# w2 laid out as eight rows on 128 partitions, five on 64 and one on 32, in a gated attention and FFN decode kernel

## The chip, the cores and the metric

The kernel runs on one core of one Trainium2 chip. The metric is the device time of one execution in microseconds; the median of three runs is 344.23 us (344.19 to 344.23). The profile is of one execution, taken by the hardware profiler.

## What is computed

One decode step for two sequences (B = 2, one new token each). An attention block with 32 heads of 128 over a cache of 4,096 keys and values, and a ReLU feed-forward block, are mixed by a gate:

```python
g = sigmoid((x * gate_w).sum(-1, keepdims=True))          # x: [2, 1, 512]
q = x @ wq                                                # wq: [512, 4096]
p = softmax(q k^T / sqrt(128))                            # k_cache, v_cache: [2, 32, 4096, 128]
a = (p v) @ wo                                            # wo: [4096, 512]
b = relu(x @ w1) @ w2                                     # w1: [512, 1376], w2: [1376, 512]
out = g * a + (1 - g) * b
```

All arrays are bf16. The inputs are 145 MB, nearly all of it the two caches, and each byte is used once.

## The kernel before

The program is written out by hand, one list of operations per engine. A helper (`P.add`) records each operation with the markers it waits for, and `emit` (line 61) turns markers into waits on one semaphore per engine; every DMA transfer has a semaphore of its own or one shared with transfers that never overlap with it. Nothing is scheduled by a compiler: an engine does its list in order.

**The transfers.** All large loads are issued by SyncE (SP) and go through one queue (q1) in this order: w1 (line 267), wq (268), ten pieces of the key cache (272), nine of the value cache (282), wo in two parts (283, 284), then w2 (285, 290). A key or value transfer waits only until its place in SBUF has been read, and several are always under way. A transfer to 128 partitions is handled by all 16 DMA engines, eight partitions each, and adds one to its semaphore for each engine that has finished, so the waiter sees 16 when all have. x and the gate's vector (lines 265, 266) go through ScalarE's own queue.

**The attention.** For each of 64 pieces of K, VectorE transposes 32x32 blocks (`k_turn`, line 386; the first one waits for pe_h, the end of the matmuls of line 371) and TensorE adds scores into four PSUM banks (lines 407 and 197). The softmax follows over all units at once (413 to 432), then nine V jobs: GpSimd, VectorE and ScalarE spread the probabilities (`spread`, 444 to 448), TensorE does 64 or 32 matmuls (461), VectorE extracts the diagonal blocks (467, 471) into X2. `o_gather` (486 to 499) normalises, `project` (508) multiplies with wo, and DVE copies the result (511).

**The feed-forward block.** Right after the query projection `ffn_h` (line 371) computes h transposed: 11 column blocks of w1, each of 128 columns, four matmuls per block, into 22 PSUM columns. VectorE (line 375, once per sequence) applies the ReLU and the gate's (1 - g) and writes hT, 128 partitions x 11 x 2. The second product needs the same split of the 1,376 hidden units: w2's first 1,280 rows are laid as ten consecutive rows on each of 128 partitions, and the eleventh block is rows 1,248 to 1,375, one row per partition. 32 of its rows (1,248 to 1,279) are in the ten already, so GpSimd zeroes their part of hT (line 379).

w2 is loaded last, into the space of the K tiles, once the last probabilities have been spread (marker pt_8). It comes as six transfers: w2a (line 285, the eleventh block, 128 x 512 elements), then (line 290) w2b with rows 0 to 5 of each partition's ten, w2c with rows 6, 7 and half of 8, w2d with half of row 9, w2e with the other half of row 8, w2f with the rest of row 9.

The end of the program, in TensorE's order: `project` (32 matmuls, line 508), four matmuls on the eleventh block (516), `wo_sum` (540, four matmuls that add the projected attention, waiting for DVE's copy of line 511), rows 0 to 7 (516, 32 matmuls; the first waits for w2b, row 6 for w2c), two matmuls for half of row 8, and `ffn_last` (520), whose six loads of weights (202) and six matmuls (208) wait for w2d, w2e and w2f. Two copies by DVE and two by ACT (579, 581) go to out_sb, and SP and ACT send one output row each (293).

Of the kernel before, what the change touches and what calls it, by code (L numbers as in the profile page):

```python
# [3 lines left out]
dt = mybir.dt  # L4
ALU = mybir.AluOpType
ACT = mybir.ActivationFunctionType
AX = mybir.AxisListType
# [78 lines left out]
def bass_gated_mix__gqa_block_cached__dense_activation_relu__decode_kernel(  # L86
# [14 lines left out]
    sb = nc.alloc_sbuf_tensor  # L101
# [3 lines left out]
    x_sb = sb("x_sb", [3, 512], dt.bfloat16)  # L105
    xT3 = sb("xT3", [128, 4, 4], dt.bfloat16)
# [7 lines left out]
    gm = sb("gm", [128, 2], dt.float32)  # L114
# [14 lines left out]
    selx = sb("selx", [128, 56], dt.float32)  # L129
# [2 lines left out]
    s4 = sb("s4", [32, 4, 128], dt.bfloat16)  # L132
    O_sb = sb("O_sb", [32, 2, 128], dt.bfloat16)
    oW = sb("oW", [128, 32, 2], dt.bfloat16)
    hT = sb("hT", [128, 11, 2], dt.bfloat16)
    out_sb = sb("out_sb", [2, 512], dt.bfloat16)


    flat = kt[:, :, :].rearrange("p k n -> p (k n)")
    kt16 = flat.bitcast(dt.bfloat16).rearrange("p (k r n two) -> p k r n two", k=NKT, r=64, two=2)  # L140
    w1 = flat[:, 0:2752].bitcast(dt.bfloat16)
    E = flat[:, 0:2048].bitcast(dt.bfloat16)
    ET = flat[:, 4096:6144].bitcast(dt.bfloat16)
    w2f = flat[:, 0:2816].bitcast(dt.bfloat16)
    w2 = w2f.rearrange("p (r n) -> p r n", n=512)
    X2 = flat[:, 2944:4096].rearrange("p (u d) -> p u d", d=128)
# [17 lines left out]
    MISC = 7 * BANK  # L164
    G_C0 = MISC + 64
    XT_B0 = 2 * (MISC + 400)
    H_C0 = MISC + 72
    L_C0 = MISC + 96
    O_C0 = MISC + 128
    R_C0 = MISC + 256  # L170
# [4 lines left out]
    sem = {n: nc.alloc_semaphore("sem_" + n) for n in names}  # L175
# [17 lines left out]
    pool, dve, act, pe, sp = (adder(e) for e in ("pool", "dve", "act", "pe", "sp"))  # L193
# [12 lines left out]
    def held_at(e, out, lhsT, rhs, g, last):  # L206
        low = e.lower_ap
        return e.add_instruction(mybir.InstMatmult(
            start_tensor_calc=False, stop_tensor_calc=last, tile_size=(128, 32), tile_position=(0, 32 * g), ldweights=False,
            name=nc.get_next_instruction_name(), engine=mybir.EngineType.PE, ins=[low(rhs), low(lhsT)], outs=[low(out)]))  # L210
# [5 lines left out]
         waits=["c_i16z"], signal="c_i16")  # L216
# [5 lines left out]
         waits=["c_i32z"], signal="c_i32")  # L222
# [6 lines left out]
         waits=["c_s4z"], signal="c_s4")  # L229
# [2 lines left out]
    wq_in = A_wq.rearrange("(p t) n -> p (t n)", t=4)  # L232
    w1_in = B_w1.rearrange("(p t) f -> p (t f)", t=4)
    wo_in = A_wo.rearrange("(p r) n -> p (r n)", r=32)
    w2_in = B_w2[0:1280, :].rearrange("(p r) n -> p (r n)", r=10)
    k_rows = A_k_cache.rearrange("b h s d -> (b h s) d")
    v_rows = A_v_cache.rearrange("b h s d -> (b h s) d")

# [30 lines left out]
    for g, (u, halves) in enumerate(segments):  # L269
        dst = kv[:, 4, :] if len(halves) == 1 else region[:, place(g) // 2, :]  # L270
        src = unit_in(k_rows, u)[:, 16384 * halves[0]:16384 * (halves[-1] + 1)]
        sp(lambda e, g=g, dst=dst, src=src: e.dma_start(dst, src).then_inc(sem_k[g % 3], 16),
           waits=([f"kt_{last_of[g - 3]}"] if g >= 3 else ["pe_qr1"] if g == 2 else []))
    for j, (u, hf) in enumerate(jobs):
        src = unit_in(v_rows, u)
# [9 lines left out]
    sp(lambda e: e.dma_start(w2[:, 10, :], B_w2[1248:1376, :]).then_inc(sem["w2a"], 16),  # L285
       waits=[f"pt_8_{hq}" for hq in range(4)])


    for name, c0, c1 in (("w2b", 0, 3072), ("w2c", 3072, 4352), ("w2d", 4608, 4864), ("w2e", 4352, 4608), ("w2f", 4864, 5120)):
        sp(lambda e, name=name, c0=c0, c1=c1: e.dma_start(w2f[:, c0:c1], w2_in[:, c0:c1]).then_inc(sem[name], 16))  # L290

    def send(b):
# [63 lines left out]
    def q_put(g):  # L356
        b, u4 = divmod(segments[g][0], 4)
        cols = qT_ps.rearrange("p (f j s m) -> p f s j m", f=2, j=4, s=4)
        for hq in range(4):
# [2 lines left out]
                in_=cols[32 * hq:32 * hq + 32, u4 // 2, 2 * (u4 % 2):2 * (u4 % 2) + 2, :, b], func=ACT.Copy),  # L362
                waits=(["pe_q", "c_qbuf"] if g < 2 else [f"pe_sc_{last_of[g - 2]}"]), signal=f"q_{g}_{hq}")

    def ffn_h():
        for ft in range(11):
            for t in range(4):
                def fn(e, ft=ft, t=t):
                    o = t * DFF
                    cols = w1[:, o + ft:o + 1280:10] if ft < 10 else w1[:, o + 1248:o + 1376]  # L370
                    return e.matmul(psf(0, 128, H_C0 + 2 * ft, 2), lhsT=cols, rhs=xT3[:, t, 0:2], start=(t == 0), stop=(t == 3))
                pe(fn, dwaits=([(sem["w1"], 16)] if ft == 0 and t == 0 else []),
                   signal=("pe_h" if ft == 10 and t == 3 else None))
        for b in range(2):
            dve(lambda v, b=b: v.tensor_scalar(out=hT[:, :, b], in0=PSF[:, H_C0 + b:H_C0 + 22:2], scalar1=0.0,
                                               scalar2=gm[:, b:b + 1], op0=ALU.max, op1=ALU.mult),
                waits=["pe_h", "dve_gm"], signal=f"dve_h{b}")
# [72 lines left out]
    def v_unit(j):  # L450
# [4 lines left out]
        for m in range(n):  # L455
            t = m % 4
            waits, dwaits = [], []
            if m == 0:
# [4 lines left out]
                rhs=rows[:, m], start=(m < 4), stop=(m >= n - 4), tile_position=(0, 32 * t)),  # L463
               waits=waits, dwaits=dwaits, signal=(f"pe_v_{j}" if m == n - 1 else None))

    def v_extract(u):
# [4 lines left out]
        dve(lambda e: e.tensor_reduce(out=X2[:, u, :], in_=Y.rearrange("p (c d) -> p d c", c=4), axis=AX.X, op=ALU.add),  # L471
            waits=[f"dve_y{u}"], signal=f"dve_x{u}")

    def denominators():
# [8 lines left out]
    def o_gather(b, js, start, stop):  # L483
        for j in js:
            u, first, last = jobs[j][0] % 4, start and j == js[0], stop and j == js[-1]
            pe(lambda e, u=u, j=j, first=first, last=last: e.matmul(  # L486
                psf(0, 32, O_C0, 128), lhsT=selx[:, 24 - 8 * u:56 - 8 * u], rhs=X2[:, j, :], start=first, stop=last),
               waits=[f"dve_x{j}"] + (["dve_rinv", "dve_selx"] if first else []) + (["dve_O0"] if b else []),
               signal=(f"pe_O{b}" if last else None))
        if not stop:  # L490
            return
        dve(lambda v, b=b: v.tensor_scalar(out=O_sb[:, b, :], in0=psf(0, 32, O_C0, 128), scalar1=rinv[:, b:b + 1],
                                           scalar2=gb[0:32, b:b + 1], op0=ALU.mult, op1=ALU.mult),
            waits=[f"pe_O{b}", "dve_rinv", "dve_g"], signal=f"dve_O{b}")
        for dq in range(4):
            pe(lambda e, dq=dq, b=b: e.matmul(psf(0, 128, R_C0 + 32 * b, 32), lhsT=s4[:, dq, :], rhs=O_sb[:, b, 32 * dq:32 * dq + 32],
                                              start=(dq == 0), stop=(dq == 3), tile_position=(0, 0)),
               waits=([f"dve_O{b}", "c_s4"] if dq == 0 else []), signal=(f"pe_R{b}" if dq == 3 else None))
        dve(lambda v, b=b: v.tensor_copy(out=oW[:, :, b], in_=psf(0, 128, R_C0 + 32 * b, 32)), waits=[f"pe_R{b}"], signal=f"dve_oW{b}")

    def fin(g):
        return psf(32 * g, 32 * g + 2, FIN_B * BANK, 128)
# [8 lines left out]
        dve(lambda v: v.tensor_copy(out=YW, in_=psf(0, 128, WO_B * BANK, 512)), waits=["pe_wo"], signal="dve_yw")  # L511

    def ffn_f(r, first=False, groups=4):
        dw = {10: [(sem["w2a"], 16)], 0: [(sem["w2b"], 16)], 6: [(sem["w2c"], 16)]}.get(r, [])
        for g in range(groups):
            pe(lambda e, g=g: e.matmul(fin(g), lhsT=hT[:, r, :], rhs=w2[:, r, 128 * g:128 * g + 128],
                                       start=first, stop=False, tile_position=(0, 32 * g)),
               dwaits=(dw if g == 0 else []), waits=(["dve_h0", "dve_h1", "c_h10", "dve_z"] if first and g == 0 else []))

    def ffn_last():  # L520
        def load(r, g):
            pe(lambda e: load_at(e, hT[:, r, :], g))

        def mult(r, g, dw=(), signal=None):
            pe(lambda e: held_at(e, fin(g), hT[:, r, :], w2[:, r, 128 * g:128 * g + 128], g, r == 9), dwaits=dw, signal=signal)

        for r, g in ((9, 0), (9, 1), (8, 2), (8, 3)):
            load(r, g)
        mult(9, 0, dw=[(sem["w2d"], 16)])
        mult(9, 1, signal="pe_fin0")  # L530
        for g in (2, 3):
            mult(8, g, dw=([(sem["w2e"], 16)] if g == 2 else []))
        for g in (2, 3):
            load(9, g)
        mult(9, 2, dw=[(sem["w2f"], 16)])
        mult(9, 3, signal="pe_fin1")

    def wo_sum():
        for g in range(4):
# [75 lines left out]
```

## Time and profile before

| | |
|---|---|
| median of three runs | 344.23 us (344.19 to 344.23) |
| profiled execution, span | 342.9 us (342.95 from the first to the end of the last instruction) |
| around the span | the profile lists no other time for that execution; the median is 1.28 us above the span |
| bytes moved, mean rate | 145.61 MB, 425 GB/s |
| TensorE, VectorE, ScalarE, GpSimd busy | 58%, 52%, 7%, 6% |
| chain of work that ended last | DMA 68%, DVE 15%, PE 13% |

The page gives the busy share of each engine in 40 slices; the row "DMA" is the mean over the 16 DMA engines, a 9 being 90% or more. Its queue lines give packets, megabytes and the packets' time as a share of 16 engines' span: q1 is SyncE's queue, q10 ScalarE's, q8 and q14 bring instructions. The trace behind the page also has each packet (start, length, bytes, queue, but not which of the 16 engines) and, for each transfer, the 16 times at which its semaphore rose; these are called landings here. All times are from the span's start.

### The profile page before, as it was taken

To read this page: it belongs to the slowest core of one execution; us is meant where nothing else is said; L and a number is where in the kernel's file an instruction comes from. 1 tells how busy PE (TensorE), PEld (TensorE's weight loads), DVE (VectorE), ACT (ScalarE), POOL (GpSimd) and SP (SyncE) were. 2 spreads that over 40 slices of the span, in tenths; PEclk is the share of its full clock that TensorE was granted. 3 is DMA by queue.
4 is the path that set the end of the run, shared out by engine and by line. 5 is a ranking of instruction groups with operands and counts; after the bars stand their busy time and mean duration, and the time that the engine had idled before them with its cause. 6 is when DMAs were issued, how large, how long until landed. Compare 5 with 4: busy or idle time off the path is not lost.

```text
span 342.9 us, 2540 instructions
## 1 busy us (share of the span) xinstructions
PE 197.8 (58%) x1228; PEld 54.3 (16%) x972; DVE 178.5 (52%) x127; ACT 23.1 (7%) x71; POOL 19.9 (6%) x36
## 2 busy tenths in 40 slices
PE   0177329799969799699799337220706043150656
PEld 0141001111111111111111013100303011020231
DVE  2239059899789899698999562220100103020121
ACT  1040000000000000000000240000000000000000
POOL 8000000000000000000000040110100101000000
PEclk9999959989999999989999858755656756565787
DMA  8998989899998999999999999999999999998996
GB/s 348 428 489 369 482 375 482 382 474 413 438 489 367 429 443 466 392 459 390 475 420 436 461 390 420 445 466 413 443 413 445 428 428 443 413 468 382 440 401 239
DMA packets 4196, 145.61 MB, mean 425 GB/s; under 512 B 469, under 2 KB 986, under 8 KB 1242
## 3 DMA queue, kind: packets, MB, share of 16 engines
q1 hardware_dynamic: 4178, 145.46, 98.5%
q8 instruction: 8, 0.13, 0.2%
q14 instruction: 2, 0.02, 0.0%
q10 hardware_dynamic: 8, 0.00, 0.0%
HBM read 145.46 MB, written 0.00 MB: 424 GB/s over the span
## 4 chain that ended last, share of the span: by engine, by line
DMA 68%; DVE 15%; PE 13%; ACT 1%; issue 1%; POOL 0%; SPq 0%; DVEq 0%
DMA kv<-in_A_k_cache_dram 31%; DMA kv<-in_A_v_cache_dram 23%; DVE kt L386 13%; DMA kt<-in_B_w_dram 9%; PE PS L461 6%; DMA kv<-in_A_wq_dram 4%; PE PS L407 3%; PE PS L197 3%; ACT kt L428 1%; PE PS L333 1%; DVE mpad L413 1%; DVE kt L471 1%; POOL ptm L444 0%; DVE qbuf L467 0%; DVE kt L432 0%
## 5 line engine op out<-in xcount | busy, mean ns | idle before, releaser
L386 DVE STREAM_TRANSPOSE kt<-kv 128x2048 f32<-128x2048 f32 x64 | 141.2, 2274 | 22.4 <-DMA kv<-in_A_k_cache_dram 22.3
L407 PE MATMUL PS<-kt,qbuf 128*128 128x512 bf16 x256 | 105.7, 413 | 31.8 <-DVE kt L386 26.3
L197 PE MATMUL PS<-kt,qbuf 128*128 128x512 bf16 x256 | 105.1, 411 | 0.0
L461 PE MATMUL PS<-kv,ptm 128*32 128x512 bf16 x512 | 46.5, 541 | 79.0 <-DMA kv<-in_A_v_cache_dram 76.0
L467 DVE TENSOR_TENSOR qbuf<-PS,maskc 128x512 f32<-128x512 f32 x9 | 6.2, 692 | 109.0 <-PE PS L461 109.0
L407 PEld LDWEIGHTS PS<-kt,qbuf 128*128 128x128 bf16 x256 | 25.5, 100 | 139.9 <-DVE kt L386 72.7
L461 PEld LDWEIGHTS PS<-kv,ptm 128*32 128x32 bf16 x512 | 19.0, 129 | 105.1 <-issue 98.6
L444 POOL COPY ptm<-kt 32x512 bf16<-32x512 bf16 (+1 forms) x18 | 11.5, 638 | 268.7 <-DVE rsum L475 175.6
L360 ACT ACTIVATE qbuf<-PS 32x8 bf16<-32x8 bf16 x40 | 7.9, 196 | 134.2 <-PE PS L197 132.7
L448 ACT ACTIVATE ptm<-kt 32x512 bf16<-32x512 bf16 (+1 forms) x9 | 5.3, 603 | 100.1 <-PE PS L461 98.7
L471 DVE TENSOR_REDUCE kt<-qbuf 128x128 f32<-128x512 f32 x9 | 9.3, 1028 | 0.3
L428 ACT ACTIVATE kt<-PS,negm 128x512 bf16<-128x512 f32 x8 | 5.4, 696 | 30.4 <-DVE negm L424 30.4
L333 PE MATMUL PS<-kv,xTw 128*32 128x512 bf16 x32 | 3.6, 629 | 5.9 <-DMA kv<-in_A_wq_dram 5.9
L478 PE MATMUL PS<-rsum,sell 128*32 128x1 f32 x4 | 0.4, 196 | 10.1 <-DVE rsum L475 10.1
L432 DVE STREAM_TRANSPOSE kt<-kt 128x1024 bf16<-128x1024 bf16 x4 | 5.0, 1245 | 1.7 <-ACT kt L428 1.4
L348 DVE CAST qrow<-PS 128x256 bf16<-128x256 f32 x2 | 2.4, 1396 | 6.4 <-PE PS L333 6.4
L508 PE MATMUL PS<-kv,oW 128*2 128x512 bf16 x32 | 3.4, 590 | 1.4 <-DMA kv<-in_A_wo_dram 1.4
L300 PE MATMUL PS<-ident,x_sb 3*128 3x3 bf16 x4 | 0.3, 166 | 6.2 <-DMA x_sb<-in_gate_w_dram 6.2
L486 PE MATMUL PS<-kt,selx 128*32 128x128 f32 x18 | 3.4, 328 | 0.3 <-DVE kt L471 0.3
L303 DVE COPY xT<-PS 128x12 bf16<-128x12 bf16 x1 | 0.2, 169 | 6.5 <-PE PS L300 6.5
L230 POOL MEMSET ptm<- 128x4096 bf16 x1 | 3.5, 3501 | 0.0
L413 DVE TENSOR_REDUCE mpad<-PS 128x1 f32<-128x2048 f32 x1 | 2.3, 2290 | 2.1 <-PE PS L197 2.1
(64 smaller groups left out, 44.2 us busy)
## 6 DMA issues: line engine op xcount, KB each, us to landing
kv<-in_A_k_cache_dram SPq DMA_DIRECT2D x4, 4096.0 KB, 31.6
kv<-in_A_v_cache_dram SPq DMA_DIRECT2D x2, 4096.0 KB, 27.0
kv<-in_A_wq_dram SPq DMA_DIRECT2D x1, 4096.0 KB, 15.0
kv<-in_A_wo_dram SPq DMA_DIRECT2D x1, 3072.0 KB, 29.3
kt<-in_B_w_dram SPq DMA_DIRECT2D x1, 1376.0 KB, 5.8
kv<-in_A_wo_dram SPq DMA_DIRECT2D x1, 1024.0 KB, 31.3
kt<-in_B_w_dram SPq DMA_DIRECT2D x1, 768.0 KB, 31.9
kt<-in_B_w_dram SPq DMA_DIRECT2D x1, 320.0 KB, 32.3
```

The source lines that it names most:

```text
L197: return e.add_instruction(mybir.InstMatmult(start_tensor_calc=start, stop_tensor_calc=stop, tile_size=(128, 128), tile_position=(0, 0), l ...
L333: pe(lambda e, n=n, t=t: e.matmul(psf(32 * (n % 4), 32 * (n % 4) + 32, (QR_B + n // 4) * BANK, 512), lhsT=xTw[:, t, :], rhs=wq_sb[:, t, n ...
L360: act(lambda a, hq=hq: a.activation(out=qbuf[32 * hq:32 * hq + 32, g % 2, :, :, 32 + 32 * hq], in_=cols[32 * hq:32 * hq + 32, u4 // 2, 2 * ...
L386: dve(lambda v: v.transpose(out=dst, in_=pairs[:, h, 64 * rr:64 * rr + 64]), waits=([f"pe_sc_{i - NKT}"] if i >= NKT else ["pe_h"] if i == ...
L407: return e.matmul(args[0], lhsT=args[1], rhs=args[2], start=first, stop=last)
L413: dve(lambda v: v.tensor_reduce(out=mpad[:, 0:1], in_=psf(0, 128, 0, 2048), axis=AX.X, op=ALU.max), waits=["pe_sc_63", "c_mpad"], signal=" ...
L428: act(lambda a, bk=bk, e2=e2: a.activation(out=blocks[:, bk, :, 16 * e2:16 * e2 + 16], in_=psf(0, 128, bk * BANK, 512).rearrange("p (r n) ...
L444: pool(lambda e, args=args: e.tensor_copy(**args), waits=waits, signal=f"pt_{j}_{hq}")
L448: act(lambda e, args=args: e.activation(func=ACT.Copy, **args), waits=waits, signal=f"pt_{j}_{hq}")
L461: pe(lambda e, m=m, t=t: e.matmul(psf(32 * t, 32 * t + 32, V_B[j % 2] * BANK, 512), lhsT=ptm[:, j % 2, 4 * m:4 * m + 4, :, :], rhs=rows[:, ...
L467: dve(lambda e: e.tensor_tensor(out=Y.rearrange("p (c d) -> p c d", c=4), in0=psf(0, 128, V_B[u % 2] * BANK, 512).rearrange("p (c d) -> p ...
L471: dve(lambda e: e.tensor_reduce(out=X2[:, u, :], in_=Y.rearrange("p (c d) -> p d c", c=4), axis=AX.X, op=ALU.add), waits=[f"dve_y{u}"], si ...
```

## The change

The 1,376 rows of w2 are split without overlap: 1,024 rows as eight per partition on 128 partitions, 320 rows as five per partition on the first 64, and 32 rows as one on each of the first 32. h follows the same split: 14 column blocks instead of 11 (eight of 128 columns, five of 64, one of 32), so 56 small matmuls instead of 44, and three VectorE operations over both sequences instead of two; the zeroing on GpSimd is gone. The second product has 14 rows instead of 11, the last six with 64 or 32 partitions.

The five rows on 64 partitions are loaded by eight transfers of eight partitions, 5,120 bytes each: partitions b, b + 4, ..., b + 28 for b = 0 to 3 and 32 to 35. The one row is loaded by transfers of 12, 10, 6 and 4 partitions, 1,024 bytes each. These twelve take w2a's place in SyncE's order and share its semaphore, which is waited for at 192. w2b has four rows per partition instead of six (columns 0 to 2,047 instead of 0 to 3,071), w2c two and a half as before, w2d to w2f a half row each as before. The six rows on 64 and 32 partitions are multiplied ahead of `wo_sum` (24 matmuls instead of four), rows 0 to 5 behind it (24 instead of 32).

w2 needs 14 rows' width in the space of the K tiles, so five of X2's nine parts move to a buffer of their own, and the output is assembled in the first two partitions of x_sb.

```diff
-    hT = sb("hT", [128, 11, 2], dt.bfloat16)
-    out_sb = sb("out_sb", [2, 512], dt.bfloat16)
+    hT = sb("hT", [128, 14, 2], dt.bfloat16)
+    X2a = sb("X2a", [128, 5, 128], dt.float32)
+    out_sb = x_sb[0:2, :]
...
-    w2_in = B_w2[0:1280, :].rearrange("(p r) n -> p (r n)", r=10)
+    w2_in = B_w2[0:1024, :].rearrange("(p r) n -> p (r n)", r=8)
+    w2_mid = B_w2[1024:1344, :].rearrange("(p r) n -> p (r n)", r=5)
...
-    sp(lambda e: e.dma_start(w2[:, 10, :], B_w2[1248:1376, :]).then_inc(sem["w2a"], 16),
-       waits=[f"pt_8_{hq}" for hq in range(4)])
-    for name, c0, c1 in (("w2b", 0, 3072), ("w2c", 3072, 4352), ("w2d", 4608, 4864), ("w2e", 4352, 4608), ("w2f", 4864, 5120)):
+    ready = [f"pt_8_{hq}" for hq in range(4)]
+    few = [(w2f[b:b + 29:4, 4096:6656], w2_mid[b:b + 29:4, :]) for b in (0, 1, 2, 3, 32, 33, 34, 35)]
+    few += [(w2[p0:p1, 13, :], B_w2[1344 + p0:1344 + p1, :]) for p0, p1 in ((0, 12), (12, 22), (22, 28), (28, 32))]
+    for i, (dst, src) in enumerate(few):
+        sp(lambda e, dst=dst, src=src: e.dma_start(dst, src).then_inc(sem["w2a"], 16), waits=ready if i == 0 else [])
+    for name, c0, c1 in (("w2b", 0, 2048), ("w2c", 2048, 3328), ("w2d", 3584, 3840), ("w2e", 3328, 3584), ("w2f", 3840, 4096)):
         sp(lambda e, name=name, c0=c0, c1=c1: e.dma_start(w2f[:, c0:c1], w2_in[:, c0:c1]).then_inc(sem[name], 16))
...
-        for b in range(2):
-            dve(lambda v, b=b: v.tensor_scalar(out=hT[:, :, b], in0=PSF[:, H_C0 + b:H_C0 + 22:2], scalar1=0.0,
-                                               scalar2=gm[:, b:b + 1], op0=ALU.max, op1=ALU.mult),
-                waits=["pe_h", "dve_gm"], signal=f"dve_h{b}")
-        pool(lambda g: g.memset(hT[0:32, 10, :], 0.0), waits=["dve_h0", "dve_h1"], signal="c_h10")
+        for i, (r0, r1) in enumerate(((0, 8), (8, 13), (13, 14))):
+            n = h_rows(r0)
+            dve(lambda v, r0=r0, r1=r1, n=n: v.scalar_tensor_tensor(
+                out=hT[0:n, r0:r1, :], in0=psf(0, n, H_C0 + 2 * r0, 2 * (r1 - r0)).rearrange("p (r b) -> p r b", b=2), scalar=0.0,
+                in1=gm[0:n, :].unsqueeze(1).to_broadcast([n, r1 - r0, 2]), op0=ALU.max, op1=ALU.mult),
+                waits=["pe_h", "dve_gm"], signal=f"dve_h{i}")
...
-        dw = {10: [(sem["w2a"], 16)], 0: [(sem["w2b"], 16)], 6: [(sem["w2c"], 16)]}.get(r, [])
+        dw = {8: [(sem["w2a"], 192)], 0: [(sem["w2b"], 16)], 4: [(sem["w2c"], 16)]}.get(r, [])
...
-    ffn_f(10, first=True)
+    ffn_f(8, first=True)
+    for r in range(9, 14):
+        ffn_f(r)
     wo_sum()
-    for r in range(8):
+    for r in range(6):
         ffn_f(r)
-    ffn_f(8, groups=2)
+    ffn_f(6, groups=2)
     ffn_last()
```

More of the change, by code (lines that the diff above doesn't have):

```diff
@@ L143, in bass_gated_mix__gqa_block_cached__dense_activation_relu__decode_kernel @@
     ET = flat[:, 4096:6144].bitcast(dt.bfloat16)
-    w2f = flat[:, 0:2816].bitcast(dt.bfloat16)
+    w2f = flat[:, 0:3584].bitcast(dt.bfloat16)
     w2 = w2f.rearrange("p (r n) -> p r n", n=512)
-    X2 = flat[:, 2944:4096].rearrange("p (u d) -> p u d", d=128)
+    X2b = flat[:, 3584:4096].rearrange("p (u d) -> p u d", d=128)
     qflat = qbuf[:, :, :, :, :].rearrange("p s e j c -> p (s e j c)").bitcast(dt.float32)
@@ L166, in bass_gated_mix__gqa_block_cached__dense_activation_relu__decode_kernel @@
     XT_B0 = 2 * (MISC + 400)
-    H_C0 = MISC + 72
+    H_C0 = MISC
     L_C0 = MISC + 96
@@ L363, in q_put, with h_rows @@
                 waits=(["pe_q", "c_qbuf"] if g < 2 else [f"pe_sc_{last_of[g - 2]}"]), signal=f"q_{g}_{hq}")
+    def h_rows(r):
+        return 128 if r < 8 else 64 if r < 13 else 32
     def ffn_h():
-        for ft in range(11):
+        for ft in range(14):
             for t in range(4):
@@ L369, in fn @@
                     o = t * DFF
-                    cols = w1[:, o + ft:o + 1280:10] if ft < 10 else w1[:, o + 1248:o + 1376]
-                    return e.matmul(psf(0, 128, H_C0 + 2 * ft, 2), lhsT=cols, rhs=xT3[:, t, 0:2], start=(t == 0), stop=(t == 3))
+                    c0, c1, step = (ft, 1024, 8) if ft < 8 else (1016 + ft, 1344, 5) if ft < 13 else (1344, 1376, 1)
+                    return e.matmul(psf(0, h_rows(ft), H_C0 + 2 * ft, 2), lhsT=w1[:, o + c0:o + c1:step], rhs=xT3[:, t, 0:2],
+                                    start=(t == 0), stop=(t == 3))
                 pe(fn, dwaits=([(sem["w1"], 16)] if ft == 0 and t == 0 else []),
-                   signal=("pe_h" if ft == 10 and t == 3 else None))
-        for b in range(2):
-            dve(lambda v, b=b: v.tensor_scalar(out=hT[:, :, b], in0=PSF[:, H_C0 + b:H_C0 + 22:2], scalar1=0.0,
-                                               scalar2=gm[:, b:b + 1], op0=ALU.max, op1=ALU.mult),
-                waits=["pe_h", "dve_gm"], signal=f"dve_h{b}")
-        pool(lambda g: g.memset(hT[0:32, 10, :], 0.0), waits=["dve_h0", "dve_h1"], signal="c_h10")
+                   signal=("pe_h" if ft == 13 and t == 3 else None))
+        for i, (r0, r1) in enumerate(((0, 8), (8, 13), (13, 14))):
[4 more added lines that the diff above has]
+                waits=["pe_h", "dve_gm"], signal=f"dve_h{i}")
     def k_turn(i):
@@ L464, in v_unit, with x2 @@
                waits=waits, dwaits=dwaits, signal=(f"pe_v_{j}" if m == n - 1 else None))
+    def x2(j):
+        return X2a[:, j, :] if j < 5 else X2b[:, j - 5, :]
     def v_extract(u):
@@ L470, in v_extract @@
             waits=[f"pe_v_{u}", "dve_maskc"] + ([f"dve_x{u - 1}"] if u else []), signal=f"dve_y{u}")
-        dve(lambda e: e.tensor_reduce(out=X2[:, u, :], in_=Y.rearrange("p (c d) -> p d c", c=4), axis=AX.X, op=ALU.add),
+        dve(lambda e: e.tensor_reduce(out=x2(u), in_=Y.rearrange("p (c d) -> p d c", c=4), axis=AX.X, op=ALU.add),
             waits=[f"dve_y{u}"], signal=f"dve_x{u}")
@@ L486, in o_gather @@
             pe(lambda e, u=u, j=j, first=first, last=last: e.matmul(
-                psf(0, 32, O_C0, 128), lhsT=selx[:, 24 - 8 * u:56 - 8 * u], rhs=X2[:, j, :], start=first, stop=last),
+                psf(0, 32, O_C0, 128), lhsT=selx[:, 24 - 8 * u:56 - 8 * u], rhs=x2(j), start=first, stop=last),
                waits=[f"dve_x{j}"] + (["dve_rinv", "dve_selx"] if first else []) + (["dve_O0"] if b else []),
@@ L513, in ffn_f @@
     def ffn_f(r, first=False, groups=4):
-        dw = {10: [(sem["w2a"], 16)], 0: [(sem["w2b"], 16)], 6: [(sem["w2c"], 16)]}.get(r, [])
+        dw = {8: [(sem["w2a"], 192)], 0: [(sem["w2b"], 16)], 4: [(sem["w2c"], 16)]}.get(r, [])
+        n = h_rows(r)
         for g in range(groups):
-            pe(lambda e, g=g: e.matmul(fin(g), lhsT=hT[:, r, :], rhs=w2[:, r, 128 * g:128 * g + 128],
+            pe(lambda e, g=g: e.matmul(fin(g), lhsT=hT[0:n, r, :], rhs=w2[0:n, r, 128 * g:128 * g + 128],
                                        start=first, stop=False, tile_position=(0, 32 * g)),
-               dwaits=(dw if g == 0 else []), waits=(["dve_h0", "dve_h1", "c_h10", "dve_z"] if first and g == 0 else []))
+               dwaits=(dw if g == 0 else []), waits=(["dve_h2", "dve_z"] if first and g == 0 else []))
     def ffn_last():
@@ L524, in mult @@
         def mult(r, g, dw=(), signal=None):
-            pe(lambda e: held_at(e, fin(g), hT[:, r, :], w2[:, r, 128 * g:128 * g + 128], g, r == 9), dwaits=dw, signal=signal)
-        for r, g in ((9, 0), (9, 1), (8, 2), (8, 3)):
+            pe(lambda e: held_at(e, fin(g), hT[:, r, :], w2[:, r, 128 * g:128 * g + 128], g, r == 7), dwaits=dw, signal=signal)
+        for r, g in ((7, 0), (7, 1), (6, 2), (6, 3)):
             load(r, g)
-        mult(9, 0, dw=[(sem["w2d"], 16)])
-        mult(9, 1, signal="pe_fin0")
+        mult(7, 0, dw=[(sem["w2d"], 16)])
+        mult(7, 1, signal="pe_fin0")
         for g in (2, 3):
-            mult(8, g, dw=([(sem["w2e"], 16)] if g == 2 else []))
+            mult(6, g, dw=([(sem["w2e"], 16)] if g == 2 else []))
         for g in (2, 3):
-            load(9, g)
-        mult(9, 2, dw=[(sem["w2f"], 16)])
-        mult(9, 3, signal="pe_fin1")
+            load(7, g)
+        mult(7, 2, dw=[(sem["w2f"], 16)])
+        mult(7, 3, signal="pe_fin1")
     def wo_sum():
```

## The prediction

> **What bounds it now.** I read the page's slices and queue lines first, then the chain of work that ended last, then SyncE's issues, and last the packet records and landings of the trace.
>
> ```profile
> DMA  8998989899998999999999999999999999998996
> ...
> q1 hardware_dynamic: 4178, 145.46, 98.5%
> q8 instruction: 8, 0.13, 0.2%
> q14 instruction: 2, 0.02, 0.0%
> ```
>
> The 16 DMA engines are busy from the first slice to the last. Followed packet by packet, each engine's stream on q1 has no gap from 1.8 us to 340.5 us, except where an instruction packet of q8 or q14 stands in it. So the kernel ends when the fullest engine has worked off its share, plus a short tail. The end of the chain of work (start, length, what) shows that tail:
>
> ```profile
> 307.33 0.33 SPq L285
> 307.65 0.04 issue
> 307.70 0.43 SPq L290
> 308.13 0.04 issue
> 308.17 32.26 DMA kt<-in_B_w_dram
> 340.43 0.04 issue
> 340.47 0.33 PE PS L516 x10
> 340.80 0.44 PE PS L208 x6
> 341.24 0.02 issue
> 341.27 0.28 DVE out_sb L579
> ```
>
> The w2 transfers are issued at 307 and land some 32 us later, behind v and wo. The last one (w2f) lands at 340.97 and the span ends at 342.95, so 1.98 us of matmuls, copies and output follow. The median of the runs is 344.23, 1.28 us over the profiled span; I carry differences in the span over to it unchanged.
>
> The engines do not finish together. Landings of the first and the last w2 transfer, one time for each of 16 engines (whole microseconds only where they change):
>
> ```
> w2a 335.72 .74 .99 336.06 .09 .13 .35 | 336.98 | 337.44 .45 .56 .59 .60 .62 .63 .73
> w2f 339.09 .20 .31 .43 .44 .47 .64 | 340.31 | 340.78 .81 .82 .85 .86 .88 .89 .97
> ```
>
> Seven are early, one is in the middle, eight are late by some 1.5 us. The packet records say why: eight packets of 16,384 B on q8 (TensorE's instructions, one per some 256 of them) fell on eight different engines and held each for 1.0 to 1.1 us, with about 0.5 us more in the packet behind it (2,880 to 2,967 ns for 65,536 B that otherwise take 2,420). Two packets of 8,192 B on q14, at 118.4 and 167.7 us, held two more engines for about 1.0 and 0.7 us; the first is the engine in the middle. Nothing ever makes that up, since no stream runs dry.
>
> **The parts of the change.** Prices per engine: packets of 11,008 B follow each other every 410 ns, of 32,768 B every 1,210 ns, so a packet costs 5 ns and 1 ns per 27.2 B; 1,024 B (42.5 ns), 2,560 (98.5) and 512 (23.5) fit. That gives 156 ns for the new 4,096 B and 193 ns for 5,120 B. A semaphore packet costs 6 ns.
>
> Removed from every engine: w2a's eight rows (8 x 42.5 + 6 = 346 ns) and, since w2b shrinks from 6,144 B to 4,096 B per partition, 8 x (235 - 156) = 632 ns. Together -0.98 us. w2c to w2f keep their sizes.
>
> Added: eight transfers of eight rows of 5,120 B. That a transfer of few rows uses only as many engines is seen in x: its two rows are two packets at the same moment (1.67 and 1.68 us). So eight rows go to eight engines, one packet each; if they are the same eight each time, these get 8 x (193 + 6) = 1.59 us. The transfers of 12, 10, 6 and 4 rows put four packets on four of these, three on two, two on two (49 ns each with their semaphore: 0.19, 0.15, 0.10 us), and two, one or none on the rest. Net: eight engines **+0.71 to +0.81 us**, the other eight **-0.88 to -0.98 us**.
>
> Which eight, the trace of before does not say: its packets carry no engine's name. [...]
>
> Now the sum. At best the eight relieved engines are exactly the eight late ones: they end at 340.97 - 0.88 or earlier, about 340.0. But nine engines are behind and only eight are relieved. The middle one then is among the loaded: 340.31 + (0.71 to 0.81) = 341.02 to 341.12, 0.05 to 0.15 us after today's 340.97. The early seven end at 339.64 + 0.81 = 340.45 or before. So the last landing hardly moves: **+0.1 us**.
>
> The rest lies beside the stream:
> - Line 371 grows from 44 to 56 small matmuls, 12 x 59 ns = 0.7 us, and line 375's two DVE operations (0.37 us) become three, at some 0.2 us each. In the rows below, the first transpose then starts near 26.8, not 25.91. The engines' queue hides it: the transfer that waits for the first four transposes is issued at 34.8 and its data are due only after the ones queued before it, at about 64. Without that cover it would cost the 0.9 us.
>
> ```profile
> 22.82 2.58 PE L371 MATMUL PS<-xT,kt 128*128 128x2 bf16 x44
> 25.44 0.37 DVE L375 TENSOR_SCALAR hT<-PS,gm 128x11 bf16<-128x11 f32 x2 [4.79 <-PE PS L371]
> 25.91 4.50 DVE L386 STREAM_TRANSPOSE kt<-kv 128x2048 f32<-128x2048 f32 x2
> ```
>
> - The memset on POOL (0.09 us) goes; nobody but the w2 matmuls waited for it.
> - Ahead of wo_sum stand 24 matmuls of line 516, not 4. 24 took 0.51 us in the tail; they start at about 338.2 to 338.5, when the small rows are there (336.98 + 1.4 on the middle engine), and end by 339.0. wo_sum waits for DVE's copy until 339.2 anyway. Cost nothing; if the rows came 0.5 us later, w2b (339.6) would still come last.
> - Behind w2c there are ten matmuls and six more, as now, so the tail stays at 1.98 us. X2's move and the output in x_sb's rows change no operation's shape.
> - SyncE issues 17 transfers, not 6: 11 more at 0.47 us (start to start), so up to 314.9 instead of 309.6, where the first w2 packet is due at 335. Hidden by 20 us, unless the queue has no room for them:
>
> ```profile
> 309.60 8.84 SPq L290 DMA_DIRECT2D kt<-in_B_w_dram  x1
> ```
>
> This last issue took 8.84 us where its sisters took 0.43. Nine transfers were then under way (two of v, two of wo, w2a to w2e), and it went through 0.61 us after the older one of v had landed on its last engine (317.83). What is full there is not shown: nine transfers, or some 81 packets per engine (nine each). By packets the small transfers cost 2 instead of 9 places, all 17 are in by about 337 at the latest, and nothing is lost. By transfers, see the third rival. Ends: 0 and +3.3 us; I take 0, because the price of a place fits packets as well and these transfers have few.
>
> [...]
>
> **Forecast:** 342.95 + 0.1 for the span, 344.23 + 0.1 = **344.35 us**, by itself 344.1 to 344.6. About 0.2% (0.69 us) is what a measurement of this kernel can tell from no change.
>
> **Rivals.**
> 1. The loaded eight hold an engine that had a q8 packet. Then the last lands at 340.78 to 340.97 plus 0.71 to 0.81, that is 0.5 to 0.8 us later: 344.8 to 345.1. For it: nothing in the trace ties the late ones to a half. Against: 40 KB moved (1.59 us) is just what separates late from early. 14%.
> 2. The middle engine does not bind, because the 8,192 B packet costs less or falls elsewhere once the programs are longer. The early seven bind: 340.45, 0.5 us sooner, 343.7. Against it: VectorE's program grows by one operation only, and the packet came at 118 us, long before the change's part. 10%. Spreading over all sixteen engines (the change not doing what it says) would give each 2 KB less, under 0.1 us, and is in the forecast's range.
> 3. On the other side: the queue takes nine transfers, whatever their size. Then the sixth of the small ones waits for v's older transfer (318.4), the seventh for the next (328.1), the eighth for wo (335.5), the first of the four for wo's rest (338.0), and the eight left take 8 x 0.47 us: w2b is issued at 339.4 and w2f by 341.8. The engines are dry from 337 on. From w1 (issued at 0.74, packets from 1.77 to 2.6) packets come 1.0 to 1.9 us after an issue's start; w2b to w2f need 2.6 us, and 0.45 to land: 343.5 to 344.3, +2.5 to +3.3 us, 346.7 to 347.5. If each engine counts for itself, the early ones free places sooner (wo's rest lands there at 335.4 to 336.0) and it is about +1.2 us, 345.5. It decides as soon as the limit counts transfers. For it: nine is what was under way. 30%.
> 4. Something else, such as a ninth q8 packet for the 48 instructions TensorE gains, near the output: 6%, up to 1 us either way.
>
> **Chances.** The forecast has 40%. Faster by over 0.2%: 0.06 (the far end of 2, and part of 4). Within 0.2%: 0.54 (forecast, most of 2, half of 1). Slower by over 0.2%: 0.40 (half of 1, all of 3, part of 4). From 343.5 to 346.7 the range holds the forecast, 1, 2 and the cheaper half of 3.
>
> **What would show it.** Right: landings of w2f in which the old late eight come about 0.9 us sooner, one engine near 341.1 is last, and the small transfers' issues are over by 337. Wrong at the step of the engines: the last landing 0.5 us or more later, with several engines there. Wrong at the queue: issues of 7 us and more among the small transfers, and slices with idle DMA between 337 and 341. Wrong at the middle engine: a last landing near 340.4.

## The result, and the profile after

| | before | after |
|---|---|---|
| median of 12 runs each, same chip | 344.26 us (344.18 to 344.47) | 345.06 us (344.92 to 345.19) |
| ratio, 95% interval | | 1.0021 (1.0013 to 1.0029) |
| profiled execution, span | 342.95 us | 343.87 us |
| last landing of w2f | 340.97 | 341.86 |
| from there to the end | 1.98 | 2.01 |

The change makes the kernel slower by 0.80 us. In the two profiled executions the difference is 0.92 us: 0.89 in the last landing, 0.03 in the tail. 344.35 had been forecast as the likeliest time; what came is rival 1, which had been put at 344.8 to 345.1.

The page of the kernel after, slices and queues first:

```profile
DMA  8998989999898999999999999999999999999995
...
q1 hardware_dynamic: 4226, 145.43, 98.3%
q8 instruction: 9, 0.15, 0.2%
q14 instruction: 2, 0.02, 0.0%
```

The DMA engines are still busy from end to end: no slice has the gap that rival 3 would have made (in the window from 337 to 340 us they are busy for 0.83 of the time, 0.84 before). A ninth q8 packet has come. It starts at 341.44, when q1 has no packet of w2 left to start (its last one starts at 341.22); the tail after it is as long as before. The end of the chain (start, length, what):

```profile
314.20 0.35 SPq L293
314.55 0.04 issue
314.60 26.62 DMA kt<-in_B_w_dram
341.21 0.04 issue
341.26 0.33 PE PS L527 x10
341.59 0.59 PE PS L209 x6
342.18 0.02 issue
342.20 0.28 DVE x_sb L592
```

It is the chain of before with other line numbers: w2c is waited for until 341.21 (before: 340.43), ten matmuls, six matmuls, copies. So one looks at the landings, one time per engine:

```
before w2f 339.09 .20 .31 .43 .44 .47 .64 | 340.31 | 340.78 .81 .82 .85 .86 .88 .89 .97
after  w2f 338.37 .51 | 339.80 .83 .84 .86 .87 .97 .99 340.15 .23 .28 | 340.65 | 341.03 | 341.69 341.86
```

Most engines have come together, between 339.8 and 340.3. But two are later than any was before, by 0.72 and 0.89 us, about the price of a loaded engine (a third, at 341.03, by 0.06); and two are earlier than any was, by 0.58 and 0.72. That looks as if work had been taken from two engines that were early and given to two that were late; the experiments test it. How the total lies, one sees from the mean of the 16 landings: 340.17 before, 340.12 after. The change moves the mean by 0.05 us only; before, the last engine was 0.80 us behind the mean, now it is 1.74 us behind.

What the timeline shows on SP, and on TensorE between the small rows and w2b:

```profile
307.16 7.00 SPq L291 DMA_DIRECT2D kt<-in_B_w_dram  x12
314.20 17.67 SPq L293 DMA_DIRECT2D kt<-in_B_w_dram  x5
...
339.64 0.60 PE L527 MATMUL PS<-kt,hT 64*2 64x128 bf16 x24 [1.14 <-DMA kt<-in_B_w_dram]
...
340.17 0.40 PE L551 MATMUL PS<-qbuf,selw 128*2 128x128 f32 x8
...
340.43 0.40 PE L527 MATMUL PS<-kt,hT 128*2 128x128 bf16 x16
```

The twelve small transfers are issued without a stop in 7.0 us. Of the five that follow, the last three take 2.5, 7.8 and 6.4 us, and the last ends at 331.87, still 5 us ahead of the first of w2b's landings (336.82). The small rows are complete at 339.60, their matmuls and `wo_sum` end at 340.57, and w2b's last engine is at 340.39.

### The profile page after: what moved, and what is told of

It is laid out like the page before. It is cut to its first block, busy times and chain, and to the rows that moved or that the text cites. A ratio compares the mean times of both kernels' runs of the same rounds, so it can differ in the third digit from the quotient of the medians.

```text
span 343.9 us, 2599 instructions
## 1 busy us (share of the span) xinstructions
PE 199.4 (58%) x1252; PEld 55.3 (16%) x996; DVE 178.1 (52%) x128; ACT 23.1 (7%) x71; POOL 19.8 (6%) x35
## 4 chain that ended last, share of the span: by engine, by line
DMA 66%; DVE 19%; PE 10%; SPq 2%; ACT 1%; issue 1%; POOL 0%; DVEq 0%
DMA kv<-in_A_k_cache_dram 31%; DMA kv<-in_A_v_cache_dram 23%; DVE kt L393 16%; DMA kt<-in_B_w_dram 8%; PE PS L468 6%; DMA kv<-in_A_wq_dram 4%; SPq L291 2%; ACT kt L435 1%; PE PS L414 1%; PE PS L198 1%; PE PS L336 1%; DVE mpad L420 1%; POOL ptm L451 0%; DVE qbuf L477 0%; DVE kt L439 0%
## 5 line engine op out<-in xcount | busy, mean ns | idle before, releaser
L468 PE MATMUL PS<-kv,ptm 128*32 128x512 bf16 x512 | 45.7, 533 | 80.4 <-DMA kv<-in_A_v_cache_dram 77.3
L481 DVE TENSOR_REDUCE X2a<-qbuf 128x128 f32<-128x512 f32 x5 | 5.1, 1028 | 0.2
L481 DVE TENSOR_REDUCE kt<-qbuf 128x128 f32<-128x512 f32 x4 | 4.1, 1025 | 0.1
L377 PE MATMUL PS<-xT,kt 128*128 128x2 bf16 (+2 forms) x56 | 3.9, 203 | 0.0
L377 PEld LDWEIGHTS PS<-xT,kt 128*128 128x128 bf16 (+2 forms) x56 | 3.9, 159 | 0.0
## 6 DMA issues: line engine op xcount, KB each, us to landing
kv<-in_A_v_cache_dram SPq DMA_DIRECT2D x2, 4096.0 KB, 27.2
```

The source lines that it names most:

```text
L377: return e.matmul(psf(0, h_rows(ft), H_C0 + 2 * ft, 2), lhsT=w1[:, o + c0:o + c1:step], rhs=xT3[:, t, 0:2], start=(t == 0), stop=(t == 3))
L468: pe(lambda e, m=m, t=t: e.matmul(psf(32 * t, 32 * t + 32, V_B[j % 2] * BANK, 512), lhsT=ptm[:, j % 2, 4 * m:4 * m + 4, :, :], rhs=rows[:, ...
L481: dve(lambda e: e.tensor_reduce(out=x2(u), in_=Y.rearrange("p (c d) -> p d c", c=4), axis=AX.X, op=ALU.add), waits=[f"dve_y{u}"], signal=f ...
```

## The experiments

The theory (A in the expectations): two of the eight engines that q8's packets made late are among the eight that the transfers of eight rows load, and they end last. Run 1 gives the engines numbers; those that a transfer of eight rows takes there are 0 to 7. B and C stand for rivals that do without late engines among the loaded: in B the loss comes with the small transfers themselves, in C it stays wherever the rows go. Times are medians against the kernel before on the same chip (344.31 or 344.32).

**1. Markers: which engines are late?** The kernel before, with 15 transfers of 1 to 15 rows of 64 B ahead of w2a. The engine whose stream holds 15 - e markers is called engine e from here on. If each transfer takes the engines of the next smaller one and one more, the 16 engines get 16 different numbers, and the transfer of eight rows is the one that takes 0 to 7.

```diff
+    for k in range(1, 16):
+        sp(lambda e, k=k: e.dma_start(mark[0:k, 32 * k:32 * k + 32], B_w2[0:k, 0:32]).then_inc(sem["mark"], 16),
+           waits=([f"pt_8_{hq}" for hq in range(4)] if k == 1 else []))
```

> [...] Theory A (the fullest engine sets the end, and the loaded eight hold two engines that an instruction packet had held): of the eight engines that land w2f at 340.8 or later, exactly two have a number below 8, and two engines with a number of 8 or more land among the early ones; the middle one has a number below 8. Rival B (the twelve small issues cost the time, the engines are well matched): all eight late ones have numbers 8 to 15. The time is that of before plus at most 0.2 us.

Measured, one run: 345.56 us (before: 344.31). wo's end and the number of marker packets behind it on the same engine:

```
early   334.86 to 335.36   engines 0, 2, 4, 7, 8, 15; 1 at 335.63
middle  336.04             engine 3 (the q14 packet of 118 us)
late    336.5 to 336.6     engines 9 to 14 (6, 5, 4, 3, 2 and 1 markers), 5 and 6 (10 and 9)
```

Engines 5 and 6 run at the same times, but their markers follow each other every 13 ns, and two such trains can be told apart in the packets: nine markers from 336.627 us on and ten from 336.636, so these are 6 and 5. So A's engines: two late ones are below 8, and 8 and 15, above it, were early. Trains of different lengths are there (1 to 6, 9 and 10 markers on the late engines), as they must be if each transfer takes the engines of the smaller ones and one more. Which engine of the chip a number stands for was not shown; the theory needs only which engines are among the eight. The time missed the expectation by 1 us: behind the markers 1,024 B packets took up to 973 ns (46 before) and 6,144 B up to 1,092 (239). Why is open. It also spoils the landings of w2f, on which the expectation was put; that is why wo's end, ahead of the markers, is read instead. As a way of looking, the markers cost 1.2 us themselves.

Carried over to the kernel after, every landing finds its place: 8 and 15, early and relieved, at 338.37 and 338.51; 9 to 14, late and relieved, and 0, 2, 4 and 7, early and loaded, are the ten from 339.80 to 340.28; 1 at 340.65; 3 at 341.03; 5 and 6, late and loaded, last. In that trace itself, the last two engines have eight packets of 5,120 B each, one with three of the 1,024 B packets (if those transfers go by the same numbers, only 4 and 5 have three) and one with two (of the loaded, only 6 and 7).

**2. Half the load.** The kernel after without four of the eight transfers: each loaded engine gets four packets of 5,120 B fewer. It leaves those rows of w2 out of the second product, and waits for 128 on their semaphore instead of 192.

```diff
-    few = [(w2f[b:b + 29:4, 4096:6656], w2_mid[b:b + 29:4, :]) for b in (0, 1, 2, 3, 32, 33, 34, 35)]
+    few = [(w2f[b:b + 29:4, 4096:6656], w2_mid[b:b + 29:4, :]) for b in (0, 1, 2, 3)]
...
```

> The kernel after, with four of the eight transfers of eight rows left out (the part of w2 for partitions 32 to 63 of the five rows is not loaded, so that part of the product is wrong). Theory A: the eight loaded engines lose 4 x 0.2 us, so the last two land near 341.06 instead of 341.86, and the time falls by 0.8 us to 344.3. Rival B (issues): eight issues instead of twelve, a third of the 0.8 us, 344.8. Rival C (layout): 345.06, no change.

Measured: 344.20 us, ratio 0.9996 (0.9987 to 1.0005), and the last two landings, alone behind the rest (340.14), at 340.82 and 340.96 instead of 341.69 and 341.86. That is 0.87 and 0.90 less for four packets of 5,120 B (four of 196 ns with their semaphore packets of 6 ns are 0.81). The end follows the load of these two engines. C is out, since the layout is the same, and so is B, which would have left 344.8 with eight small transfers.

**3. Other instruction packets.** The kernel after without the second half of each V matmul loop (the attention sums over part of the keys only). That is 512 instructions fewer on TensorE.

```diff
-        n = 64 if hf is None else 32
+        n = 32 if hf is None else 16
```

> The kernel after, with the second half of the matmuls of each V job left out (the values of half of the keys are loaded but not multiplied), so that TensorE's program is 512 instructions shorter, two blocks of 256. Theory A (an engine is late because a 16,384 B instruction packet stood in its stream): seven q8 packets instead of nine, six of them ahead of w2 instead of eight, and two engines fewer carry the delay of about 1.5 us. If one of the released engines is among the lowest eight, only one of the two last landings stays near 341.8; if both are, the last landing is near 341.0 and the time 344.2; if neither is, the time stays 345.06. Rival (the lateness belongs to the engine or its place, not to the packets): the same landings as after.

Measured: 345.02 us (344.14 to 345.52), ratio 1.0019 (1.0009 to 1.0028). The page has two instruction packets fewer on q8 than after had:

```profile
q8 instruction: 7, 0.11, 0.1%
q14 instruction: 2, 0.02, 0.0%
```

and four relieved engines now are early where there were two, while the last two are where they were to within 0.2 us:

```
w2f 338.37 .43 .46 .74 | 339.90 .93 .94 .99 340.11 .12 .13 .19 | 340.73 | 340.98 | 341.51 341.89
```

So being late is no property of an engine: 512 instructions less make two engines less late. In this pair of runs two q8 packets go with these 512 instructions of TensorE, one of 16,384 B with 256 (after: nine packets, 0.15 MB; here: seven, 0.11 MB). Here both late engines that got free were in the upper half, so that the last landing didn't move. The time by itself shows less than its median suggests: the ten executions spread over 1.4 us, and the profiled one is the longest of them (tail 2.23 us, granted clock 0.77 against 0.82 of the kernel after). Where the packets fell in the others is not known.

**4. The same rows on all 16 engines.** One transfer of 64 partitions for the five rows, one of 32 for the single one.

```diff
-    few = [(w2f[b:b + 29:4, 4096:6656], w2_mid[b:b + 29:4, :]) for b in (0, 1, 2, 3, 32, 33, 34, 35)]
-    few += [(w2[p0:p1, 13, :], B_w2[1344 + p0:1344 + p1, :]) for p0, p1 in ((0, 12), (12, 22), (22, 28), (28, 32))]
+    few = [(w2f[0:64, 4096:6656], w2_mid), (w2[0:32, 13, :], B_w2[1344:1376, :])]
...
```

> The kernel after, but the five rows come in one transfer of 64 partitions (four packets of 5,120 B on each of 16 engines) and the one row in one transfer of 32 partitions (two packets of 1,024 B each). Theory A (the fullest engine sets the end): against before each engine loses 0.98 us and gets 4 x 0.193 + 0.006 and 2 x 0.043 + 0.006 us, so the last landing is 0.1 us earlier than before, near 340.86, and the time 344.15. Rival B (twelve small issues cost): also near before, 344.2 to 344.3. Rival C (the layout itself costs: 14 row blocks, more TensorE instructions, the ninth instruction packet): 345.0 as after.

Measured: 345.82 us, ratio 1.0043 (1.0031 to 1.0056); last landing 342.54. Every theory missed, A too. The windows of 337 to 340 us and 340 to 342 us of the kernel after, then of this run, show why (length, busy time of PE, PEld, DVE, ACT and POOL, granted clock, DMA's busy share, GB/s):

```profile
337.00:340.00 3.00, 1.86 (x36) 0.43 (x28) 0.69 (x1) 0.00 (x0) 0.00 (x0) 0.79 0.83 299
340.00:342.00 2.00, 1.57 (x52) 0.68 (x44) 0.26 (x1) 0.26 (x1) 0.00 (x0) 0.92 0.14 41
```

```profile
337.00:340.00 3.00, 1.18 (x12) 0.10 (x8) 0.69 (x1) 0.00 (x0) 0.00 (x0) 0.50 1.01 247
340.00:342.00 2.00, 1.80 (x52) 1.14 (x56) 0.00 (x0) 0.00 (x0) 0.00 (x0) 0.50 0.63 219
```

The engines are fully busy and move less: 247 GB/s at a share of 1.01, against 299 at 0.83. (A share can pass 1 because an engine's packets overlap by some ns: 1,024 B take 46 ns and follow each other every 42.) The packets themselves are slow. 5,120 B took 308 ns (median, up to 399) instead of 196; wo's 8,192 B beside them up to 625 instead of 312.

**5. The same in twelve pieces.** Eight column pieces of 640 B on 64 partitions, four of 256 B on 32.

```diff
-    few = [(w2f[b:b + 29:4, 4096:6656], w2_mid[b:b + 29:4, :]) for b in (0, 1, 2, 3, 32, 33, 34, 35)]
-    few += [(w2[p0:p1, 13, :], B_w2[1344 + p0:1344 + p1, :]) for p0, p1 in ((0, 12), (12, 22), (22, 28), (28, 32))]
+    few = [(w2f[0:64, 4096 + c:4096 + c + 320], w2_mid[:, c:c + 320]) for c in range(0, 2560, 320)]
+    few += [(w2[0:32, 13, c:c + 128], B_w2[1344:1376, c:c + 128]) for c in range(0, 512, 128)]
```

> As the spread version, but in twelve issues: the five rows in eight column pieces of 64 partitions x 640 B, the one row in four of 32 partitions x 256 B, so that all 16 engines get the same. Theory A (the fullest engine): 8 x (4 x 0.0285 + 0.006) = 0.96 and 4 x (2 x 0.0145 + 0.006) = 0.14 us in the place of 0.98: last landing 0.1 us later than before, 344.4. Rival B (the number of issues): 345.0 as after, since there are as many. Rival C (the layout): 345.0.

Measured: 346.72 us, ratio 1.0068 (1.0055 to 1.0081); last landing 343.05. Missed in the same way: 640 B packets took 48 ns (median, up to 107), where 5 ns and 1 ns per 27.2 B give 28.5.

**6. Neighbouring partitions.** Does the place of the rows in SBUF make packets slow? The kernel after with the same eight transfers on the same eight engines, each to eight partitions side by side instead of four apart.

```diff
-    few = [(w2f[b:b + 29:4, 4096:6656], w2_mid[b:b + 29:4, :]) for b in (0, 1, 2, 3, 32, 33, 34, 35)]
+    few = [(w2f[b:b + 8, 4096:6656], w2_mid[b:b + 8, :]) for b in range(0, 64, 8)]
```

> The kernel after, but each of the eight transfers of eight rows goes to eight neighbouring partitions (8b to 8b + 7) instead of every fourth one. Number of transfers, engines and bytes are the same. [...] Rival (the spread version was slow for the reading side or for having 16 engines on few rows): no change, 345.06.

Measured: 346.79 us, ratio 1.0074 (1.0057 to 1.0091), so 1.7 us more than the kernel after, for the same bytes on the same engines. The 5,120 B packets took 300 ns (median, up to 440) instead of 196, and the last landing came at 343.08, 1.22 later. So the rival's 345.06 is out. On 64 neighbouring partitions from 16 engines they had taken 308 (run 4). Why they are slow was not shown. What is shown is that the same rows on the same engines are slow when they are taken side by side. This edit changes both ends: the rows are neighbours in HBM too, and no run separates reading from writing. Against the reading side speaks the kernel before, where w2a reads 128 rows of 1,024 B that lie side by side in HBM into 128 partitions: 46 ns a packet, one every 42, which is just 5 ns and 1 ns per 27.2 B. Nor are neighbouring partitions always slow: the 32 packets of 1,024 B in the kernel after go to such partitions, and took 46 to 49 ns.

**7. Load only engines that are early.** Engines 0 to 2 were early (run 1). The kernel before with its ten rows on 128 partitions, but the last 96 rows without w2a's overlap, as eight rows on each of 12 partitions, by four transfers of three partitions ahead of wo. Their eight matmuls (512 wide, 12 partitions) stand in the middle of `project`, all on one tile position.

```diff
+    w2_few = B_w2[1280:1376, :].rearrange("(p r) n -> p (r n)", r=8)
...
+    for b in range(4):
+        sp(lambda e, b=b: e.dma_start(kv[b:b + 9:4, 3, 0:4096], w2_few[b:b + 9:4, :]).then_inc(sem["w2a"], 16))
...
+            if r == 15:
+                for c in range(8):
+                    pe(lambda e, c=c: e.matmul(psf(0, 2, WO_B * BANK, 512), lhsT=hT[0:12, 10 + c, :], rhs=kv[0:12, 3, 512 * c:512 * c + 512],
+                                               start=False, stop=False, tile_position=(0, 0)),
+                       dwaits=([(sem["w2a"], 64)] if c == 0 else []), waits=(["dve_h1"] if c == 0 else []))
```

> A layout from theory A and the engine numbers read so far (late: 5, 6, 9 to 14; in the middle 3, a little behind 1): w2 as ten rows on 128 partitions, as before, and the other 96 rows as eight per partition on twelve partitions, by four transfers of three rows of 8,192 B to partitions b, b + 4, b + 8, so that only the engines 0, 1 and 2 get them. They come ahead of wo, and their eight matmuls go into the bank of the projection. Every engine loses w2a's 0.346 us, the engines 0 to 2 get 4 x 0.313 us. Theory A: the late eight land 0.35 us sooner (340.62 at the last), engines 0 to 2 near 340.4 to 340.6, time 343.9. Rival (more row blocks, more small transfers or the ninth instruction packet cost by themselves): 344.3 or more.

Measured: 347.96 us, ratio 1.0104 (1.0088 to 1.0119). The last landing came 0.1 us behind the 340.62 that was expected (340.72), but the end hung on TensorE. Its timeline:

```profile
336.90 3.57 PE L513 MATMUL PS<-kv,hT 12*2 12x512 bf16 x8
...
340.40 1.88 PE L508 MATMUL PS<-kv,oW 128*2 128x512 bf16 x16
...
342.33 0.69 DVE L516 COPY qbuf<-PS 128x512 f32<-128x512 f32 x1 [8.13 <-PE PS L508]
```

On one tile position the eight matmuls run one after the other, 0.43 us each at a granted clock of 0.50 (336 to 340 us), and push `project`'s second half and DVE's copy (338.48 before) back to 342.33.

**8. The same, with the eight matmuls out of the way.** They stand ahead of `project`, over all four tile positions.

```diff
+        for c in range(8):
+            t = c % 4
+            pe(lambda e, c=c, t=t: e.matmul(psf(32 * t, 32 * t + 2, WO_B * BANK, 512), lhsT=hT[0:12, 10 + c, :], rhs=kv[0:12, 3, 512 * c:512 * c + 512],
+                                            start=(c < 4), stop=False, tile_position=(0, 32 * t)),
+               dwaits=([(sem["w2a"], 64)] if c == 0 else []), waits=(["dve_h1", "dve_z"] if c == 0 else []))
```

> As the run before it (ten rows of w2 on 128 partitions, the last 96 as eight on each of 12 partitions, loaded by four transfers of three partitions ahead of wo), but the eight matmuls of those 96 rows stand ahead of project's 32, spread over the four tile positions, in the time in which TensorE waits for wo. Streams: unchanged, last landing about 340.6 to 340.8 (340.72 in the run before). Theory (only TensorE's tail spoilt the run before): the tail behind the last landing is 2.0 us again, span 342.6 to 342.8, time 343.9 to 344.1, that is 0.2 to 0.4 us below the kernel before. Rival (the row blocks and the four transfers cost something by themselves, in wo's packets or in project): 344.3 or more, with project's end or wo's landings later than in the kernel before.

Measured: 344.15 us, before 344.32, ratio 0.9995 (0.9986 to 1.0004); span 342.85, last landing 340.78, tail 2.07. The timeline:

```profile
334.31 0.60 PE L507 MATMUL PS<-kv,hT 12*2 12x512 bf16 x8
...
335.15 1.47 PE L513 MATMUL PS<-kv,oW 128*2 128x512 bf16 x24 [0.24 <-DMA kv<-in_A_wo_dram]
...
338.20 0.69 DVE L516 COPY qbuf<-PS 128x512 f32<-128x512 f32 x1 [3.58 <-PE PS L513]
```

The eight matmuls now take 0.60 us in TensorE's wait for wo, and the copy is at 338.20 again. The time lies 0.05 us above the theory's range and well inside what can't be told from no change, so this run does not prove a gain. Nor did all three loaded engines prove early. Followed packet by packet, two of them land w2f at 340.11 and 340.15, amid the rest; the third, 0.6 us behind these two already at its first extra row (326.00), is the last at 340.78, where 340.4 to 340.6 had been expected. The engines at 340.75 and 340.77 got none of the extra rows: when an earlier v transfer landed they were 0.3 us behind the other late ones (317.90, the next at 317.56). So who is late, and by how much, is not quite the same in this kernel. What the run shows is that these four transfers to three engines cost nothing that can be measured, where the change, with its transfers to 0 to 7, cost 0.80 us.

## Why the prediction was right and wrong

- **The time: inside the range by its width.** 345.06 lies within 343.5 to 346.7 because that range also holds rivals 1 and 2 and half of rival 3. The case that was held likeliest (344.35, 40%) did not come; rival 1 (14%) did.
- **What bounds the kernel: right.** The streams of the DMA engines, without gaps, and an unchanged tail (1.98 predicted, 2.01).
- **The price of a loaded and a relieved engine: nearly right.** The first landing behind the two early ones is at 339.80, just the 340.78 of the first late engine less the 0.98 of relief; the middle one came 0.72 later (340.31 to 341.03; predicted 341.02 to 341.12). The last one (6, with two small rows) stands 0.89 above the last of before, where 0.71 had been worked out for such an engine. On that engine the packets of 5,120 and 4,096 B followed each other every 200 and 157 ns (mean) instead of the 193 and 156 taken, eight of each, which is 0.07 us; and the last landing of wo, ahead of the new transfers, was already 0.10 later (337.46 after 337.36).
- **The same eight engines for all eight transfers, and the small rows on the same ones:** a term of the sum that no row of before shows. In the trace of after the two engines that end last have eight packets of 5,120 B each, with three and two of 1,024 B, and the two that end first have none of 5,120 B; run 2, with four of the transfers left out, moves the last two landings by 0.87 and 0.90 us.
- **The middle engine among the loaded: right**, and of no weight, since others were behind it.
- **"At best the eight relieved engines are exactly the eight late ones": this is the step that failed.** The sum went on from this best case. Six of eight late engines were relieved (9 to 14); 5 and 6 were loaded. The prediction had the right price for that (rival 1) and gave it 14%, because the 40 KB that are moved equal the gap between late and early. That agreement is of sizes; it says nothing of which engines. By the trace of before, any eight of 16 could have been the late ones, and a single one of them in the wrong half was enough for rival 1. If one set of eight is as likely as another, the best case is one of 12,870, so it was the case that needed a reason.
- **The small rows: wrong in size, without effect.** They were complete at 339.60, not 338.2 to 338.5, because the last of them comes on the late loaded engines. `wo_sum` moved from 339.23 to 340.17. Nothing waited for it: w2b, itself 0.78 later, landed at 340.39, and its matmuls start at 340.43.
- **SP's issues: wrong in size, hidden.** 0.62 to 0.76 us for each of the eight instead of 0.47. The last one ended at 331.87, within the 337 given.
- **The queue: right.** Sixteen transfers were under way when w2b was issued (two of v, two of wo, the twelve small ones), and it took 0.35 us. A limit of nine transfers (rival 3, 30%) does not exist here; the stalls of w2d to w2f fit a limit by packets, and cost nothing. (An estimate from the transfers under way: 78 packets on an engine with four small rows when w2d stalled, 81 when w2f stalled before, 72 when w2e did not.)
- **The ninth q8 packet (rival 4):** it came, at 341.44, and cost nothing that shows.

What stays open: why q8's packets fall on 5, 6 and 9 to 14, why packets behind the 64 B markers were slow (run 1), and why packets to partitions side by side were (runs 4 to 6).

## What to carry to other kernels

Every DMA engine's stream is full here, and the time followed the fullest engine (in run 2 the last landing came 0.90 us sooner and the time fell by 0.86). What balancing can bring is then bounded by one subtraction: the last landing less the mean of the 16, here 0.80 us or 0.23% (the change's fewer bytes lowered that mean by only 0.05). Before bytes are moved from one set of engines to another, show which engines are late; a split that fits in size may still be wrong by place, and a change of the program can change which engines are late (runs 3 and 8). Eight transfers of eight partitions put their bytes on the same eight engines here; with partitions four apart the 5,120 B packets took 196 ns, side by side 300.

## What was not expected of the hardware

- Packets of 5,120 B to 64 neighbouring partitions, or to eight side by side, took 300 to 308 ns where the same bytes four partitions apart took 196, and packets of another transfer beside them up to 625 instead of 312.
- A 16,384 B instruction packet (1.0 to 1.1 us, with some 0.5 us more behind it) stays in an engine's account to the end: one on each of eight engines from 30 us on still shows as 1.5 us at 341 us.
- A transfer of 8 partitions of 5,120 B took SP 0.62 us to issue, one of 128 partitions 0.33 to 0.43 where it did not stall (2.5 to 8.8 where it did, before and after).
- Eight matmuls of 512 columns took 3.57 us on one tile position and 0.60 on four (runs 7 and 8). Part of it is the granted clock, 0.50 to 0.52 from 334 to 340 us in the first and 0.98 to 1.00 in the second; that is a factor of two, and three is left for the tile positions and for whatever else differs between the two runs, as an estimate. Why the clock differed is open.
